# New costs in the scheduler of an attention and two-MLP kernel: loads, small operations, maxima, changes of TensorE's division; the first unit's loads ahead of the third's

## The chip, the cores and the metric

The kernel runs on one core of a Trainium2 chip. A core has five engines that work beside each other, each through its own instructions in order: TensorE (PE, matrix products), VectorE (DVE), ScalarE (ACT), GpSimd (POOL), and SyncE (SP), which here issues loads and stores. The metric is the device time of one execution in microseconds (us). The median is over the runs of a kernel; less is better.

## What is computed

Causal softmax attention is mixed with a linear memory by a gate for each head, and the result goes through two MLPs; all inputs are float32. Here B = 4, H = 8, S = 576, D = 64, and there are B x S = 2304 tokens of 512 numbers.

```python
def _attn_ref(q, k, v, M_prev, z_prev, beta):
    scores = scale * np.matmul(q, k.transpose(0, 1, 3, 2))   # scale = 1 / sqrt(D)
    scores = np.where(causal, -1000000000.0, scores)
    a = np.exp(scores - scores.max(-1, keepdims=True))
    a /= a.sum(-1, keepdims=True) + 1e-09
    local = np.matmul(a, v)
    q_p = phi(q)                                             # phi(x) = (x > 0 ? x : exp(x) - 1) + 1
    mem_ret = np.einsum('bhsd,bhde->bhse', q_p, M_prev)
    mem_norm = np.einsum('bhsd,bhd->bhs', q_p, z_prev)[..., None] + 1e-06
    g = 1.0 / (1.0 + np.exp(-beta))[None, :, None, None]
    return g * (mem_ret / mem_norm) + (1 - g) * local

def _moe_ref(x, w_in, w_out, s, b):         # 512 -> 2048 -> 512
    r = np.maximum(x @ w_in, 0.0)
    return (s * (r * r) + b) @ w_out

def _moe2_ref(x, w_in, w_out, a, b):        # 512 -> 2048 -> 512
    h = x @ w_in
    P = a[0] + a[1] * h + a[2] * h**2 + a[3] * h**3
    Q = 1.0 + np.abs(b[0]) * np.abs(h) + np.abs(b[1]) * h**2
    return (P / (Q + 1e-06)) @ w_out
```

## The kernel before

**The work and its names.** Attention is cut into 32 units: four batches, times two ranges of query rows (rows 0 to 2 and rows 3 to 4, in tiles of 128), times four pairs of heads. A unit with number p loads `q`, `k`, `vm` (v, scaled to `vs` on arrival), `qm` (the queries by rows) and, for two units together, `zb` (z_prev for all partitions). PE forms the scores `s` (line 648), DVE their maxima `st` (655, a custom operation with a second one that reads its accumulator), ACT the exponentials `p` with row sums `rs` (666). PE transposes `p` to `pt` (525), ACT or DVE copies them to `th`, and PE multiplies by `vs` into `av` (857). The memory term goes over `ph` (phi of qm), `tz` = ph x zb (378), the reduction `c` (591), a scaled `ph`, its transpose `pf`, its copy `fs` (for some units also the remainder `fl`), and the last product into `av` (865), which reads `qm` itself as memory. `xp` = av x `cb` (868) ends the unit; `cb` holds reciprocal row sums, for units from 4 on over a round trip through DRAM (store `crow`, load `cb`). Rows of x leave for a DRAM tile `xTd`.

Weights arrive as raw pieces of 128x512 values, two words each (`dAi_0r`, `dAi_1r` of the first MLP's input weights, `dAo0r` to `dAo7r` of its output weights). DVE and ACT decode each: ACT squares (`m`, 418), DVE runs 419, 421, 423 and 425 into `f`; then a high part (`w1ihA`, `w1ohA`, a cast) and a low part (`w1ilA`, `w1olA`, a subtraction at 378) are kept, so that PE multiplies in three passes. `ha` (913) and `acc` (978) are the first MLP's two products for seven blocks of tokens whose x is early; they are mixed into the attention. Activations there are `ra`, `gha` and `gla`. The blocks after them and the whole second MLP follow the attention (`hb`, `ab`, `hc`, `ac`).

**What sets the order.** No order is written by hand. Code adds operations to a plan, each with its due time `at`, the tiles that it reads and writes, and a table `ways` of its cost on each engine that may do it. `Plan.run` then plays the kernel through in its own clock: it takes again and again the operation that can start first (ties go by `at`), on the engine where it would end first, adds its cost to that engine's clock, and frees its consumers after a gap from the table `GAPS`. What comes out is one fixed list of instructions for each engine, which the chip then runs in order; costs never appear in a run, they only decide order and engine. Waits at run time are semaphores on real completions.

Costs come from `ways()` (a base plus columns times a rate), `small()` for operations of a few columns, `pe()` for TensorE, and `load()` for transfers. Most loads go through SP, in order, with a clock step of 0.48 for each; a load of a tile also waits until the buffer's last reader is done, and each of SP's eight queue lanes takes a new load only when the one eight places earlier has landed. The keys of the first units and the gate (`beta`) are loaded by ACT. `gates()` turns beta into `gate`, `omg` and `gate2` by small operations on DVE. PSUM has eight banks: a tile that opens a bank waits until its last reader frees it.

`prepare_qk(p)` loads q and k of a unit, `prepare(p)` its vm, qm and zb. The first three units have their q and k due at TS - AHEAD + 0.001 p, ahead of the rest of their loads; the gate at 0.0005.

Of the kernel before, what the change touches and what calls it, by code (L numbers as in the profile page):

```python
# [20 lines left out]
P = 128  # L21
# [19 lines left out]
PCOPY = False  # L41
RAW = 0
ALONE = 8
R0, R1, RN = 0.0, 0.0, 0
ENDS, LEAD, LEADS = 1, 0.7, 384
WIDTHS = 512, 512, 512, 384, 384
D0, D1, D2, D3 = 10.0, 8.0, 3.0, 0.0
TINYPOOL = 0.12
DIRECT, GATE, MPLAIN = 4, 1.0, 4
# [10 lines left out]
class Op:  # L60


    def __init__(self, ways, fn, at):
        self.ways, self.fn, self.at = ways, fn, at
        self.left, self.next, self.ready, self.end = 0, [], {e: 0.0 for e in ways}, 0.0
        self.touch, self.opens, self.port = [], [], False

# [12 lines left out]
class Plan:  # L80
# [83 lines left out]
    def run(self, engines, nbanks):  # L164
        clock = {e: 0.0 for e in engines}
        wait = {e: [] for e in engines}
        bank_free, bank_of = [0.0] * nbanks, [None] * nbanks
        dma, busy, port = 0.0, [], 0.0
        wait_for = [WAIT_AT]
# [35 lines left out]
        for _ in self.ops:  # L205
            cand = [(c[1], c[2].at, e, c[2], c[3]) for e, c in ((e, choose(e)) for e in engines) if c is not None]
            start, _, e, o, b = min(cand, key=lambda c: c[:2])
            for x in o.ways:
                wait[x].remove(o)
            cost = o.ways[e]  # L210
            if e == "PE":
                busy = [x for x in busy if x[1] > start - 4.0]
                if sum(y - max(x, start - 4.0) for x, y in busy) < 2.6:
                    cost *= 2
                busy.append((start, start + cost))
            elif e != "SP":
                cost *= INFL
            if e == "SP":
                clock[e] = start + 0.48
                dma = max(dma, start + 1.2) + cost  # L220
                o.end = dma + 1.2
            else:
                clock[e] = start + cost
                o.end = clock[e] + o.lag
                if e == "POOL" or e == "DVE" and o.port:
                    port = clock[e]
            for t, i in zip(o.opens, b):
                bank_of[i] = t
                t.obj = self.pools["ps"].tile(t.shape, t.dt, tag=f"bank{i}", name=t.name)
            o.start, o.eng = start, e  # L230
            if o is self.swap:
                wait_for[0] = WAIT
            o.fn(engines[e])
            for t in o.touch:
                t.left -= 1
                t.free = max(t.free, o.end)
                if not t.left and t.place is not None and t.place[0] == "ps":
                    i = bank_of.index(t)
                    bank_of[i], bank_free[i] = None, t.free + BGAP
            for n in o.next:  # L240
# [8 lines left out]
def tile_kernel(ctx, tc, qk, vm, z, beta, w1i, w1o, s1, b1, w2i, w2o, a2, b2, out):  # L249
# [106 lines left out]

    def load(dst, src, size, r=(), w=(), act=False):

        if act:
            op({"ACT": 0.55}, lambda e: e.dma_start(dst(), src()), r, w, lag=1.7 + size / 360e3)  # L360
        else:
            op({"SP": 0.1 + size / 350e3}, lambda e: e.dma_start(dst(), src()), r, w)  # L362
# [17 lines left out]
    def small(fn, r, w, ways_=("DVE", "POOL")):  # L380

        t = {"DVE": 0.07, "POOL": TINYPOOL}
        op({e: t[e] for e in ways_}, fn, r, w, port="POOL" in ways_)

    def pe(cols, fn, r, w, n=0):

        op({"PE": cols * 0.000422 + n * 0.0135}, lambda e: fn(), r, w)

    def gates():

        load(lambda: gate, lambda: beta.rearrange("(o h) -> o h", o=1).to_broadcast([P, H]), 5e3, (), ("gate",), True)
        op(ways(H, 0.0), lambda e: e.activation(gate, gate, AF.Exp, scale=-1.0), ("gate",), ("gate",))
        op(ways(H, None, 1.0), lambda e: e.tensor_scalar(gate, gate, 1.0, None, ALU.add), ("gate",), ("gate",))
        op(ways(H, None, 1.0), lambda e: e.reciprocal(gate, gate), ("gate",), ("gate",))
        op(ways(H, None, 1.0), lambda e: e.tensor_scalar(omg, gate, -1.0, 1.0, ALU.mult, ALU.add), ("gate",), ("omg",))
        op(ways(H, None, 1.0), lambda e: e.tensor_copy(gate2[:, :, 0], gate), ("gate",), (("gate2", 0),))
        for j in range(2):
            m = slice(64 * j, 64 * j + 64)
            op(ways(H, None, 1.0), lambda e, j=j, m=m: e.tensor_copy(gate2[m, j::2, 1], gate[m, j::2]), ("gate",), (("gate2", 1 + j),))


# [136 lines left out]
    def diagonal(p):  # L538

        Q, QD = f"q{p}", f"qd{p % 2}"  # L540
        for j in range(2):
            m = slice(j * D, j * D + D)
            op({"POOL": 0.2}, lambda e, m=m: e.tensor_scalar(g(QD)[m, m], g(Q)[m, P:P + 64], 1.0, 0.0, ALU.mult, ALU.add),
               (Q,), ((QD, j),))

    def prepare(p):
# [6 lines left out]
        if r.ta == 0:  # L553
            load(lambda: g(f"vm{p}")[:, 0:r.kb], lambda: tiles[:, 0:r.kb], P * 512 * r.kb, (), (f"vm{p}",))
            load(lambda: g(f"qm{p}"), lambda: tiles[:, NQ:NQ + 4], P * 512 * 4, (), (f"qm{p}",))
# [66 lines left out]
    def scores(p):  # L622
# [7 lines left out]
        for i, (cols, pieces) in enumerate(r.scores):  # L630
# [6 lines left out]
            for t, x, ka, kb, o in pieces:  # L637
# [11 lines left out]

                pe(4.9 * (kb - ka), mm, (Q, K), [(b, t) for b in banks], 7)  # L650
                for n, b in zip(ns, banks):
# [7 lines left out]
                    ST = (f"st{n}", t)  # L659
                    op(ways(kb - ka, None, 1.0), top, ((b, t), ST) if x else ((b, t),), ((b, t), ST))  # L660
                todo.append((t, x, ka, kb, o, banks, o2))
# [9 lines left out]
    def scores_last(p):  # L671
# [4 lines left out]
        for x in range(2):  # L676
# [4 lines left out]
            def mm(SB=SB, ks=ks):  # L681
                nc.tensor.matmul(g(SB)[:, 0:QB], g(Q), g(K)[:, ks], start=True, stop=True)  # L682

            pe(4.5 * QB, mm, (Q, K), (SB,))
            op(ways(QB, None, 1.0), lambda e, SB=SB, x=x: e.tensor_tensor_reduce(
                g(SB)[:, 0:QB], g(SB)[:, 0:QB], mask2 if x else mask[:, 0:QB], -scale,
# [154 lines left out]
    def values(p, runs):  # L841
# [17 lines left out]

        pe(2 * sum(x[6] - x[5] for x in part) + 50 * len(part), mm, sorted({x[3] for x in part}) + [VS], (AV,))  # L860

# [310 lines left out]
    for j in range(n_early):  # L1172
# [176 lines left out]
```

## Time and profile before

| what | us |
|---|---|
| median of 3 runs (lowest, highest) | 1061.24 (1059.4, 1061.42) |
| the profiled execution, whole time | 1060.15 |
| its span, first to last instruction | 1058.4 |
| busy: PE, DVE, ACT, POOL | 1016.3, 849.0, 687.5, 414.9 |

The span is the part of an execution in which instructions run; 1.75 us of the profiled one lie outside it. A busy time is the sum in which an engine has at least one instruction running. The mean granted clock of TensorE was 0.985 of full speed. The attention with the weight decodes and the first token blocks takes about the first 400 us; the rest is the two MLPs.

### The profile page before, as it was taken

To read this page: it belongs to the slowest core of one execution; us is meant where nothing else is said; L and a number is where in the kernel's file an instruction comes from. 1 tells how busy PE (TensorE), PEld (TensorE's weight loads), DVE (VectorE), ACT (ScalarE), POOL (GpSimd) and SP (SyncE) were. 2 spreads that over 40 slices of the span, in tenths; PEclk is the share of its full clock that TensorE was granted. 3 is DMA by queue.
4 is the path that set the end of the run, shared out by engine and by line. 5 is a ranking of instruction groups with operands and counts; after the bars stand their busy time and mean duration, and the time that the engine had idled before them with its cause. 6 is when DMAs were issued, how large, how long until landed. Compare 5 with 4: busy or idle time off the path is not lost.

```text
span 1058.4 us, 17508 instructions
## 1 busy us (share of the span) xinstructions
PE 1016.3 (96%) x5980; PEld 868.7 (82%) x5980; DVE 849.0 (80%) x1511; ACT 687.5 (65%) x1449; POOL 414.9 (39%) x470
## 2 busy tenths in 40 slices
PE   5886999999999999999999999999999999999998
PEld 3565888878888789987778999888888888898997
DVE  5999987888779885479999543888888888887896
ACT  5866666676557653355554443877866877777895
POOL 2423221032002211012021002877777876876785
PEclk8998999999999999999999999999999999999999
DMA  6666566666656655986765332900200200010000
GB/s 196 203 191 189 150 194 207 170 201 192 192 158 187 181 176 174 365 254 206 254 204 194 102 99 65 325 1 1 78 1 0 70 1 1 23 41 1 30 1 31
DMA packets 88633, 140.42 MB, mean 133 GB/s; under 512 B 12408, under 2 KB 50400, under 8 KB 88544
## 3 DMA queue, kind: packets, MB, share of 16 engines
q1 hardware_dynamic: 83856, 130.52, 39.0%
q0 software_dynamic: 4224, 8.39, 2.5%
q8 instruction: 47, 0.77, 0.3%
q10 hardware_dynamic: 464, 0.40, 0.1%
q14 instruction: 42, 0.34, 0.1%
HBM read 103.56 MB, written 35.71 MB: 132 GB/s over the span
## 4 chain that ended last, share of the span: by engine, by line
PE 71%; DVE 13%; DMA 8%; ACT 3%; issue 2%; SPq 2%; POOL 0%; ACTq 0%; DVEq 0%; POOLq 0%
PE hc L913 19%; PE ac L1104 19%; PE ab L1017 7%; PE hb L913 7%; PE ha L913 6%; PE acc L978 6%; SPq L362 2%; PE av L857 2%; PE pt L525 2%; PE s L648 1%; DVE s L655 1%; DMA cb<-crow 1%; PE av L865 1%; DMA dAi_0r<-in_w1i 1%; PE su L682 1%
## 5 line engine op out<-in xcount | busy, mean ns | idle before, releaser
L1083 DVE RECIPROCAL qe<-qe 128x512 f32<-128x512 f32 (+2 forms) x82 | 242.6, 2959 | 49.4 <-POOL qe L378 49.4
L913 PE MATMUL hc<-xc_h,w2ih 128*128 128x512 f32 (+1 forms) x320 | 117.8, 368 | 0.0
L913 PE MATMUL hc<-xc_h,w2il 128*128 128x512 f32 (+1 forms) x320 | 117.8, 368 | 0.0
L913 PE MATMUL hc<-xc_l,w2ih 128*128 128x512 f32 (+1 forms) x320 | 117.7, 368 | 0.0
L378 POOL TENSOR_TENSOR qe<-qe,qb 128x512 f32<-128x512 f32 (+2 forms) x82 | 94.9, 1158 | 55.1 <-ACT qb L1068 54.2
L1104 PE MATMUL ac<-w2oh,ghc 128*128 128x512 f32 x288 | 112.6, 391 | 0.0
L1104 PE MATMUL ac<-w2ol,ghc 128*128 128x512 f32 x288 | 112.5, 391 | 0.0
L1104 PE MATMUL ac<-w2oh,glc 128*128 128x512 f32 x288 | 112.3, 390 | 0.0
L378 POOL TENSOR_TENSOR glc<-po,ghc 128x512 fp32r<-128x512 f32 (+2 forms) x82 | 95.0, 1158 | 23.2 <-ACT ghc L368 23.1
L378 POOL TENSOR_TENSOR pm<-pm,s 128x512 f32<-128x512 f32 (+2 forms) x82 | 95.3, 1162 | 17.1 <-ACT pm L1068 16.2
L525 PE MATMUL pt<-ident,p 128*128 128x128 f32 x320 | 62.0, 291 | 24.0 <-DVE xp L868 6.8
L1074 ACT ACTIVATE s<-hc 128x512 f32<-128x512 f32 (+2 forms) x82 | 44.6, 544 | 61.2 <-PE hc L913 58.3
L978 PE MATMUL acc<-gha,w1olA 128*128 128x256 f32 x288 | 83.7, 291 | 0.0
L978 PE MATMUL acc<-gla,w1ohA 128*128 128x256 f32 x288 | 81.5, 283 | 0.1
L978 PE MATMUL acc<-gha,w1ohA 128*128 128x256 f32 x288 | 81.3, 282 | 0.0
L666 ACT ACTIVATE p<-s,st 128x128 f32<-128x128 f32 (+3 forms) x128 | 66.5, 526 | 21.7 <-DVE st L655 20.4
L1068 ACT ACTIVATE pm<-hc,prm 128x512 f32<-128x512 f32 (+2 forms) x82 | 59.6, 726 | 22.4 <-DVE hc L1085 21.9
L525 PEld LDWEIGHTS pt<-ident,p 128*128 128x128 f32 x320 | 40.8, 147 | 38.9 <-ACT th L368 8.6
L913 PEld LDWEIGHTS hc<-xc_h,w2il 128*128 128x128 f32 x320 | 60.1, 188 | 9.1 <-DVE po L1087 0.4
L913 PEld LDWEIGHTS hc<-xc_l,w2ih 128*128 128x128 f32 x320 | 60.1, 188 | 8.6
L913 PEld LDWEIGHTS hc<-xc_h,w2ih 128*128 128x128 f32 x320 | 60.0, 188 | 7.4
L1068 ACT ACTIVATE qb<-s,cq,b1abs 128x512 f32<-128x512 f32 (+2 forms) x82 | 62.7, 764 | 2.1 <-POOL qe L378 2.1
(493 smaller groups left out, 2979.8 us busy)
## 6 DMA issues: line engine op xcount, KB each, us to landing
vm<-in_vm SPq DMA_DIRECT2D x16, 384.0 KB
k<-in_qk SPq DMA_DIRECT2D x32, 144.0 KB
x2p<-ev SPq DMA_DIRECT2D x18, 256.0 KB
out_y<-ob SPq DMA_DIRECT2D x18, 256.0 KB
qm<-in_vm SPq DMA_DIRECT2D x16, 256.0 KB
w1d<-sh SPq DMA_DIRECT2D x16, 256.0 KB
w1d<-sl SPq DMA_DIRECT2D x16, 256.0 KB
w2d<-sh SPq DMA_DIRECT2D x16, 256.0 KB
```

Of the source, the lines that this page charges most:

```text
L362: op({"SP": 0.1 + size / 350e3}, lambda e: e.dma_start(dst(), src()), r, w)
L378: op(ways(c, None, dve, pool), lambda e: e.tensor_tensor(dst(), x(), y(), alu), r, w, port=True)
L525: nc.tensor.transpose(dst[:, o:o + P], src, ident)
L666: e.activation(g(f"p{n}_{i}")[:, o:o + kb - ka], g(b)[:, o2:o2 + kb - ka], AF.Exp, scale=-1.0, bias=g(f"st{n}")[:, z_:z_ + 1], accum_out=g ...
L857: nc.tensor.matmul(g(AV)[64 * j:64 * j + 64, ra:rb], g(VS)[:, kb, j], g(TH)[:, o:o + rb - ra], start=x in firsts, stop=False, skip_group_c ...
L913: nc.tensor.matmul(hs(), m, y, start=c == 0 and k == 0, stop=c == KC - 1 and k == 2)
L978: nc.tensor.matmul(a, outp(y, f)[:, cs], g(z_)[:, us], start=f == 0 and k == 0 and c % 2 == 0, stop=f == HF - 1 and k == 2, skip_group_che ...
L1017: nc.tensor.matmul(g(ACC)[:, 0:w], outp(y, f)[:, cs], g(z_), start=f == 0 and k == 0, stop=f == HF - 1 and k == 2)
L1068: return lambda e: e.activation(g(dst)[:, ks], g(src)[:, ks], AF.Identity, scale=m, bias=b)
L1074: op(ways(c, -0.04), lambda e, ks=ks: e.activation(g(S2)[:, ks], g(HS)[:, ks], AF.Square), (HS,), part(S2))
L1083: op({"DVE": 0.07 + c * 0.00625}, lambda e, ks=ks: e.reciprocal(g(QE)[:, ks], g(QE)[:, ks]), part(QE), part(QE))
L1104: nc.tensor.matmul(g(ACC), g(x_)[:, ks], g(f"w2o{y}{i}")[:, o], start=f == 0 and q == 0, stop=f == NF - 1 and q == 2)
```

## The change

The diff changes numbers with which the plan reckons, and the code order of a few loads. No operation is added, taken away or made different.

- Engines' clocks no longer all start at 0 in the plan, but at FIRST (DVE at 2.0, POOL at 3.7). A load costs SP 0.64 instead of 0.48 as long as the plan is before 12 us.
- Small operations cost 0.12 on DVE (0.07 before) and 0.22 on POOL (0.12); maxima cost 0.03 more, those of the last scores 0.06 more; a block of qd costs POOL 0.25 (0.2); a load on ACT costs 0.62 (0.55), the gate's load lands 1.0 later and its exponential costs 1.3 more. The rest of the gate's operations isn't planned before 8.6.
- TensorE operations have a mark `split`: scores "rows", the products with vs "columns", others none. Where the mark changes, unless there was none before, the plan adds 0.2.
- The third unit's q and k are due at 0.02 instead of 0.002, so behind the first unit's `prepare` (0.01). In `prepare`, units with query rows 0 to 2 load vm behind qm and zb instead of ahead of them.

```diff
+FIRST = {"PE": 0.0, "ACT": 0.72, "DVE": 2.0, "POOL": 3.7, "SP": 0.73}
+ISSUE, SLOWLY, UNTIL, TABLE, BEYOND, GATES = 0.48, 0.64, 12.0, 1.3, 1.0, 8.6
...
-TINYPOOL = 0.12
+TINYPOOL, TINYDVE, TOPS, LEAVE = 0.22, 0.12, 0.03, 0.2
...
-        clock = {e: 0.0 for e in engines}
+        clock = dict(FIRST)
...
+                if split is not None and o.split != split:
+                    cost += LEAVE
+                split = o.split
...
-                clock[e] = start + 0.48
+                clock[e] = start + (SLOWLY if start < UNTIL else ISSUE)
...
-            op({"ACT": 0.55}, lambda e: e.dma_start(dst(), src()), r, w, lag=1.7 + size / 360e3)
+            op({"ACT": 0.62}, lambda e: e.dma_start(dst(), src()), r, w, lag=1.7 + late + size / 360e3)
...
-        t = {"DVE": 0.07, "POOL": TINYPOOL}
+        t = {"DVE": TINYDVE, "POOL": TINYPOOL}
...
+        plan.since = GATES
...
-                    op(ways(kb - ka, None, 1.0), top, ((b, t), ST) if x else ((b, t),), ((b, t), ST))
+                    op({"DVE": ways(kb - ka, None, 1.0)["DVE"] + TOPS}, top, ((b, t), ST) if x else ((b, t),), ((b, t), ST))
...
         if r.ta == 0:
-            load(lambda: g(f"vm{p}")[:, 0:r.kb], lambda: tiles[:, 0:r.kb], P * 512 * r.kb, (), (f"vm{p}",))
             load(lambda: g(f"qm{p}"), lambda: tiles[:, NQ:NQ + 4], P * 512 * 4, (), (f"qm{p}",))
...
+        if r.ta == 0:
+            load(lambda: g(f"vm{p}")[:, 0:r.kb], lambda: tiles[:, 0:r.kb], P * 512 * r.kb, (), (f"vm{p}",))
...
-        events.append((t - AHEAD if p >= RQ else TS - AHEAD + 0.001 * p, lambda p=p: prepare_qk(p)))
+        events.append((t - AHEAD if p >= RQ else TS - AHEAD + (0.001, 0.002, 0.02)[p], lambda p=p: prepare_qk(p)))
...
-    plan.at = TS - AHEAD + 0.0005
+    plan.at = TS - AHEAD + 0.0015
```

Three places show how the lists of instructions move; lines of the changed kernel are 5 to 8 higher. TensorE has 5,355 rows of instructions before and after, and the last 3,260 of them are the same in kind.

SP, the program's first loads. Before (a digit in a name is the unit, here 0 to 2, and the number behind it counts tiles):

```order
L362 DMA q0_155<-in_qk 64x384 x2
L362 DMA q1_161<-in_qk 64x384 x2
L362 DMA q2_167<-in_qk 64x384
L362 DMA k2_170<-in_qk 64x384
L362 DMA q2_167<-in_qk 64x384
L362 DMA k2_170<-in_qk 64x384
L362 DMA vm0_176<-in_vm 128x384
L362 DMA qm0_181<-in_vm 128x512
L362 DMA zb0_189<-in_z 128x256
L362 DMA dAi0_0r_195<-in_w1i 128x1024
L362 DMA qm1_202<-in_vm 128x512
```

After:

```order
L367 DMA q0_157<-in_qk 64x384 x2
L367 DMA q1_162<-in_qk 64x384 x2
L367 DMA qm0_168<-in_vm 128x512
L367 DMA zb0_170<-in_z 128x256
L367 DMA vm0_172<-in_vm 128x384
L367 DMA q2_178<-in_qk 64x384
L367 DMA k2_181<-in_qk 64x384
L367 DMA q2_178<-in_qk 64x384
L367 DMA k2_181<-in_qk 64x384
L367 DMA dAi0_0r_205<-in_w1i 128x1024
L367 DMA qm1_210<-in_vm 128x512
```

qm, zb and vm of unit 0 stand ahead of q and k of unit 2, and vm behind zb; the first weight piece stays in its place.

DVE, around the first instruction of the first piece's decode (`dAi0_0f`). The rows ISA on line 655 are the maxima, of unit 0 (`s0`, `s1`) and unit 1 (`s2`, `s3`). Before, from unit 0's last maximum on:

```order
L655 ISA s1_1_0_209,st1_197<-s1_1_0_209,mask_78 128x384
L655 ISA st1_197 128x1
L589 SCALAR_TENSOR_TENSOR ph0_223<-qm0_181,ph0_223 128x384
L655 ISA s2_0_0_225,st2_248<-s2_0_0_225,mask_78 128x128
L655 ISA st2_248 128x1
L378 TENSOR_TENSOR tz0_251<-ph0_223,zb0_189 128x384
L702 TENSOR_SCALAR rs0_200<-rs0_200 128x2x3
L419 TENSOR_SCALAR dAi0_0f_264<-dAi0_0r_195 128x512
L705 RECIPROCAL rec0_95<-rs0_200 128x6
L591 TENSOR_REDUCE c2_0_272<-tz0_251 128x3x2
L421 SCALAR_TENSOR_TENSOR dAi0_0f_264<-dAi0_0r_195,dAi0_0f_264 128x512
```

After, the eleven rows that end with the decode's first instruction:

```order
L663 ISA st1_187 128x1
L599 TENSOR_REDUCE c2_0_243<-tz0_213 128x3x2
L663 ISA s2_0_0_215,st2_253<-s2_0_0_215,mask_78 128x128
L663 ISA st2_253 128x1
L663 ISA s3_0_0_216,st3_256<-s3_0_0_216,mask_78 128x128
L663 ISA st3_256 128x1
L602 RECIPROCAL c2_0_243<-c2_0_243 128x6
L663 ISA s2_0_0_215,st2_253<-s2_0_0_215,mask_78 128x256
L663 ISA st2_253 128x1
L713 RECIPROCAL rec0_95<-rs0_193 128x6
L426 TENSOR_SCALAR dAi0_0f_276<-dAi0_0r_205 128x512
```

tz, the reduction c2_0 and two more maxima of unit 1 (`s3` of 128, `s2` of 256) stand ahead of the first decode instruction; before, the reduction and those maxima stood behind it.

SP, unit 4's round trip of c through DRAM. Before:

```order
L362 DMA crow4_127<-c1_4_914 2x128
L362 DMA crow4_127<-c1_4_914 2x1x64
L362 DMA qm7_934<-in_vm 128x128
L362 DMA qm7_934<-in_vm 64x128 x2
L362 DMA zb4_957<-in_z 128x256
L362 DMA k10_966<-in_qk 64x384
L362 DMA q10_912<-in_qk 64x384
L362 DMA k10_966<-in_qk 64x384
L362 DMA cb4_990<-crow4_127 64x192 x2
```

After:

```order
L367 DMA crow4_127<-c1_4_950 2x128
L367 DMA crow4_127<-c1_4_950 2x1x64
L367 DMA dAi0_1r_972<-in_w1i 128x1024
L367 DMA qm7_940<-in_vm 64x128
L367 DMA zb4_992<-in_z 128x256
L367 DMA cb4_1010<-crow4_127 64x192 x2
```

Between the store crow4 and the load cb4 stood seven loads, and now three.

## Rows read from the trace of the kernel before

**Rows 1.** The page's head: the span and PE's busy time.

```profile
span 1058.4 us, 17508 instructions
...
PE 1016.3 (96%) x5980; PEld 868.7 (82%) x5980; DVE 849.0 (80%) x1511; ACT 687.5 (65%) x1449; POOL 414.9 (39%) x470
```

**Rows 2.** Windows by stage: from:to us, length; busy us (x instructions); PEclk, DMA share, GB/s.

```profile
0.00:16.00 16.00, 7.67 (x38) 5.65 (x38) 6.11 (x30) 5.21 (x16) 3.10 (x15) 0.98 0.68 208
16.00:116.00 100.00, 82.49 (x540) 61.74 (x540) 92.62 (x250) 73.30 (x196) 30.40 (x59) 0.87 0.61 184
116.00:400.00 284.00, 273.78 (x2132) 232.77 (x2132) 230.33 (x690) 184.17 (x503) 53.47 (x109) 0.99 0.60 183
400.00:1050.00 650.00, 647.93 (x3256) 565.27 (x3255) 518.48 (x539) 422.38 (x730) 326.75 (x285) 1.00 0.31 101
```

**Rows 3.** Waits of DVE, 0 to 116 us: total us, times, longest.

```profile
DVE ph L587 <- DMA qm<-in_vm: 3.2, 2, 1.8
DVE tz L378 <- DMA zb<-in_z: 2.7, 1, 2.7
DVE xp L868 <- DMA cb<-crow: 2.0, 1, 2.0
```

**Rows 4.** Waits of PE, 0 to 120 us.

```profile
PE pt L525 <- DVE xp L868: 6.8, 1, 6.8
PE pt L525 <- ACT th L368: 6.4, 2, 5.2
```

**Rows 5.** Timeline of DVE: start, length in us; [idle before it <- its releaser].

```profile
14.70 0.56 DVE L378 TENSOR_TENSOR tz<-ph,zb 128x384 f32<-128x384 f32 x1 [2.73 <-DMA zb<-in_z]
...
16.00 0.43 DVE L419 TENSOR_SCALAR dAi_0f<-dAi_0r 128x512 int32<-128x512 int32 x1 [0.66 <-DMA dAi_0r<-in_w1i]
...
16.44 0.51 DVE L591 TENSOR_REDUCE c<-tz 128x6 f32<-128x384 f32 x1
...
17.54 0.29 DVE L655 CUSTOM_DVE_ANT_0 s<-s,mask 128x128 f32<-128x128 f32 x1
...
18.50 0.43 DVE L655 CUSTOM_DVE_ANT_0 s<-s,mask 128x256 f32<-128x256 f32 x1
...
33.88 0.36 DVE L587 TENSOR_SCALAR ph<-qm 128x384 f32<-128x384 f32 x1 [1.46 <-DMA qm<-in_vm]
...
73.43 0.36 DVE L868 TENSOR_TENSOR xp<-av,cb 128x192 f32<-128x192 f32 x1 [2.05 <-DMA cb<-crow]
...
115.43 0.68 DVE L378 TENSOR_TENSOR w1olA<-dAo7f,w1ohA 128x512 fp32r<-128x512 f32 x1
```

**Rows 6.** Timeline of SP: the issue of three loads.

```profile
7.56 0.44 SPq L362 DMA_DIRECT2D zb<-in_z  x1
...
27.97 0.33 SPq L362 DMA_DIRECT2D qm<-in_vm  x1
...
69.95 1.24 SPq L362 DMA_DIRECT2D cb<-crow  x2
```

**Rows 7.** Timeline of ACT around the first square of a weight piece.

```profile
16.00 0.68 ACT L418 ACTIVATE dAi_0m<-dAi_0r 128x512 f32<-128x512 f32 x1 [3.96 <-DMA dAi_0r<-in_w1i]
16.58 0.36 ACT L666 ACTIVATE p<-s,st 128x128 f32<-128x128 f32 x1
```

**Rows 8.** Timeline of PE: unit 0's last product.

```profile
27.13 0.81 PE L865 MATMUL av<-fs,qm 128*128 128x384 f32 x2
```

**Rows 9.** Timeline of PE: two products of the first MLP.

```profile
90.76 0.28 PE L913 MATMUL ha<-xa0l,w1ihA 128*128 128x256 f32 x1
90.88 0.28 PE L913 MATMUL ha<-xa0h,w1ihA 128*128 128x256 f32 x1
```

**Rows 10.** Waits of PE, 116 to 410 us.

```profile
PE pt L525 <- DVE fl L766: 4.5, 6, 1.4
PE pt L525 <- DVE gla L931: 2.1, 4, 1.4
```

**Rows 11.** Window after PE's longest wait, as rows 2.

```profile
96.00:106.00 10.00, 7.22 (x46) 6.46 (x47) 9.63 (x24) 5.19 (x14) 4.09 (x8) 0.60 0.45 156
```

More of the change, by code (lines that the diff above doesn't have):

```diff
@@ L65, in __init__ @@
         self.left, self.next, self.ready, self.end = 0, [], {e: 0.0 for e in ways}, 0.0
-        self.touch, self.opens, self.port = [], [], False
+        self.touch, self.opens, self.port, self.split = [], [], False, None
 class Buf:
@@ L164, in run @@
     def run(self, engines, nbanks):
-        clock = {e: 0.0 for e in engines}
+        clock = dict(FIRST)
         wait = {e: [] for e in engines}
         bank_free, bank_of = [0.0] * nbanks, [None] * nbanks
-        dma, busy, port = 0.0, [], 0.0
+        dma, busy, port, split = 0.0, [], 0.0, None
         wait_for = [WAIT_AT]
@@ L355, in ways, with load @@
         return t
-    def load(dst, src, size, r=(), w=(), act=False):
+    def load(dst, src, size, r=(), w=(), act=False, late=0.0):
         if act:
-            op({"ACT": 0.55}, lambda e: e.dma_start(dst(), src()), r, w, lag=1.7 + size / 360e3)
+            op({"ACT": 0.62}, lambda e: e.dma_start(dst(), src()), r, w, lag=1.7 + late + size / 360e3)
         else:
@@ L380, in small, with pe @@
     def small(fn, r, w, ways_=("DVE", "POOL")):
-        t = {"DVE": 0.07, "POOL": TINYPOOL}
+        t = {"DVE": TINYDVE, "POOL": TINYPOOL}
         op({e: t[e] for e in ways_}, fn, r, w, port="POOL" in ways_)
-    def pe(cols, fn, r, w, n=0):
-        op({"PE": cols * 0.000422 + n * 0.0135}, lambda e: fn(), r, w)
+    def pe(cols, fn, r, w, n=0, split=None):
+        op({"PE": cols * 0.000422 + n * 0.0135}, lambda e: fn(), r, w).split = split
     def gates():
-        load(lambda: gate, lambda: beta.rearrange("(o h) -> o h", o=1).to_broadcast([P, H]), 5e3, (), ("gate",), True)
-        op(ways(H, 0.0), lambda e: e.activation(gate, gate, AF.Exp, scale=-1.0), ("gate",), ("gate",))
+        load(lambda: gate, lambda: beta.rearrange("(o h) -> o h", o=1).to_broadcast([P, H]), 5e3, (), ("gate",), True, BEYOND)
+        op(ways(H, TABLE), lambda e: e.activation(gate, gate, AF.Exp, scale=-1.0), ("gate",), ("gate",))
+        plan.since = GATES
         op(ways(H, None, 1.0), lambda e: e.tensor_scalar(gate, gate, 1.0, None, ALU.add), ("gate",), ("gate",))
@@ L399, in gates @@
             op(ways(H, None, 1.0), lambda e, j=j, m=m: e.tensor_copy(gate2[m, j::2, 1], gate[m, j::2]), ("gate",), (("gate2", 1 + j),))
+        plan.since = 0.0
     roles = {}
@@ L542, in diagonal @@
             m = slice(j * D, j * D + D)
-            op({"POOL": 0.2}, lambda e, m=m: e.tensor_scalar(g(QD)[m, m], g(Q)[m, P:P + 64], 1.0, 0.0, ALU.mult, ALU.add),
+            op({"POOL": 0.25}, lambda e, m=m: e.tensor_scalar(g(QD)[m, m], g(Q)[m, P:P + 64], 1.0, 0.0, ALU.mult, ALU.add),
                (Q,), ((QD, j),))
@@ L648, in mm @@
                         nc.tensor.matmul(g(b)[:, o2:o2 + kb - ka], g(Q)[m, q], g(K)[m, ka:kb], start=True, stop=True)
-                pe(4.9 * (kb - ka), mm, (Q, K), [(b, t) for b in banks], 7)
+                pe(4.9 * (kb - ka), mm, (Q, K), [(b, t) for b in banks], 7, split="rows")
                 for n, b in zip(ns, banks):
@@ L684, in scores_last @@
             pe(4.5 * QB, mm, (Q, K), (SB,))
-            op(ways(QB, None, 1.0), lambda e, SB=SB, x=x: e.tensor_tensor_reduce(
+            op({"DVE": ways(QB, None, 1.0)["DVE"] + 2 * TOPS}, lambda e, SB=SB, x=x: e.tensor_tensor_reduce(
                 g(SB)[:, 0:QB], g(SB)[:, 0:QB], mask2 if x else mask[:, 0:QB], -scale,
@@ L858, in mm @@
                                  start=x in firsts, stop=False, skip_group_check=True)
-        pe(2 * sum(x[6] - x[5] for x in part) + 50 * len(part), mm, sorted({x[3] for x in part}) + [VS], (AV,))
+        pe(2 * sum(x[6] - x[5] for x in part) + 50 * len(part), mm, sorted({x[3] for x in part}) + [VS], (AV,), split="columns")
         def mem():
```

## Prediction

> **What bounds the kernel now.** I read the busy times first, then the same by stage, then the waits of the two busiest engines in the early stages, and last the order in time around each wait. PE is busy for 1016.3 of 1058.4 us [rows 1]. The stages [rows 2] tell where the other 42 us lie: 8.3 in the first 16 us, 17.5 between 16 and 116 us, 10.2 between 116 and 400, 2 between 400 and 1050, the rest in the tail. So from 400 us on nothing can be gained but by PE doing less, and the change gives PE the same 5,355 rows of instructions. Between 16 and 116 us DVE is busy for 92.6 of 100 us: there VectorE, which decodes the weights beside the attention, sets the end, and PE's gaps are mostly DVE's lateness seen from PE. From 116 us on PE is the bound again, with small gaps. A gain must therefore be (a) time in which DVE waits before 116 us, (b) work that leaves DVE there, or (c) work that PE has already done when that zone ends.
>
> DVE's waits before 116 us that the change touches [rows 3] are 3.2 us for qm, 2.7 for zb, 2.0 for cb. PE's two longest [rows 4] are 6.8 us (a transpose that needs the PSUM bank that xp frees) and 6.4 (transposes that wait for ACT's copies).
>
> **The start.** The profile of before shows DVE idle until 14.70 us for tz, whose zb was asked for at 7.56 us [rows 5, 6]; then, at 16.00, the first weight piece dAi_0r lands, and ACT's copy of unit 0's transposes is queued behind ACT's square of that piece (row dAi_0m: 3.96 us waited) [rows 7]. After the change zb and qm stand third and fourth in SP's queue, so tz, its reduction and three maxima of unit 1 come ahead of the decode's first instruction. dAi_0r stays in place 10, behind the same bytes, and the square still stands ahead of the copies, so I leave the 16.00 where it is. What DVE had to do behind 16.00 and now does before it is the reduction (0.51), a maximum of 128 (0.29) and one of 256 (0.43) [rows 5]: 1.2 us of lead. PE gets less at once: on ACT the exponential that stood between the square and the copies (16.58, 0.36 us) [rows 7] is now ahead of both, so the copies come 0.3 us earlier; but unit 0's last product is then reached without the later waits, and I let it end about 1 us earlier than its 27.13 + 0.81 = 27.94 us [rows 8]. Bounds of the term: 0.3 (the ACT step alone) to 1.2. I take 1.2 for DVE, since DVE sets this zone.
>
> **Unit 2's qm.** Its load is issued at 27.97 us, the moment unit 0's last product (which reads the same buffer) ends at 27.94, and lands at 33.88, where DVE had waited 1.46 us [rows 5, 6, 8]: 5.9 us for 256 KB, with a 512 KB weight piece ahead of it. After, it stands one place later in SP's queue, behind a vm load, but the product ends 1 us earlier and the piece ahead is asked for earlier too. If it still takes 5.9 us from some 26.9 us, it lands at 32.8, and DVE, 1.2 us ahead of 33.88 - 1.46 = 32.4, is there at 31.2: the wait stays at 1.5, and DVE keeps only 1.1 of lead. If it comes much sooner, the 1.46 us go as well. I take 1.0 us of it, because most of those 5.9 us went to the bytes ahead, and keep 0 and 1.46.
>
> A rule bears on this term. The Trainium skill (DMA: Bandwidth & Descriptors, Anatomy of one DMA) gives about 2.0 us plus the bytes over 436 KB per us for one transfer by GpSimd's software queue, an estimate of 2.6 us here. The row shows more than twice that, in a loaded queue; by the page the wait would vanish and the sum be 0.5 us lower, by the row it would stay and the sum be 1.0 higher.
>
> **cb of unit 4.** DVE waits 2.05 us for it at 73.43, and its load was issued at 69.95 [rows 5, 6]. Between the store that it reads and cb itself stood seven loads on SP; now three. A load takes SP 0.4 to 0.6 us (zb 0.44, cb 1.24 for two) [rows 6], so cb is asked for about 2 us earlier relative to its store. I take 1.5, between 0 (a queue lane that must first land an older load holds SP) and 2.05.
>
> **DVE's share of the work.** The planner also hands out movable operations anew, because small ones and maxima now cost DVE more in its tables. Counted up to the last first-layer decode (115.43 us before), DVE has one 512-wide two-input operation less (0.68 us, as w1olA) and two 384-wide products ph less (0.56 each, as tz) [rows 5]; against that stand two 256-wide products, a reduction, two scalings and an ml more, and a copy th, a copy rb and a cast less, together about 0.9 us more. Net 0.9 us less. Bounds: 0 to 1.8. Zero is real: what leaves DVE goes to POOL, which is slower at it and may run beside DVE's own two-input operations.
>
> **PE's place at the end of that zone.** When PE comes to unit 9's first scores, it has by the order done 12 ha products more and 6 transposes more, and one 256-wide and one 384-wide score product less. A ha product takes 0.12 us from start to start [rows 9]; a transpose I put at the same, the two scores at 0.35 together (estimates from that row, by columns). 18 x 0.12 - 0.35 = 1.8 us of PE's work are moved into gaps that DVE had left. This counts in full only if PE is never held afterwards; I take half, 0.9, with 0 and 1.8 as bounds.
>
> **The 6.8 us stall.** Before, PE had six ha products between unit 6's last product and the transpose that needs the bank; after, it has two score products, twelve ha and ten products of the next unit's av, some 4 us by my estimate. xp, however, stands behind much the same decodes on DVE. The gap shrinks as seen from PE, but what PE does there it lacks later in the same DVE-bound zone; it is the previous term seen from another side, and I count it once.
>
> **New waits.** Each term takes slack out of somewhere, and landings that the plan misjudged before it can misjudge at other places. DVE's three waits named above made 7.9 us; I charge a quarter of that, 2.0 us, for waits that I can't name, between 0 and 5.5 (all the gains named, which new waits would then eat).
>
> **The sum.** 1.2 + 1.0 + 1.5 + 0.9 + 0.9 - 2.0 = 3.5 us. Against the profiled execution, 1060.15 us (a span of 1058.4 and 1.75 around it), that is 1056.7. The median shown is 1061.24, 1.1 us above the profiled one; halfway between the two references gives 1057.2 us. From no change a measurement of this kernel can tell about 0.2%, 2.1 us.
>
> **Rivals.**
>
> *The gain is swallowed.* The zone is bound by DVE, dAi_0r still lands at 16.00, and the leads are only earlier arrivals at loads that come when they come: qm takes its 5.9 us, the lanes hold cb, and only content and half a microsecond of start are left. 0.3 + 0 + 0 + 0.9 + 0.9 - 1.0 = 1.1 less: 1059.6 from the same starting point (1060.7). For it: all three of DVE's named waits are for transfers, whose landing no order sets; against it: they are asked for earlier in the new order. Chance 0.22.
>
> *Slower.* PE's order from 116 to 400 us is dealt anew, too, and PE is in order: a transpose that waits for fl or gla from DVE holds all that stands behind it. Before, six waits for fl and four for gla cost 4.5 and 2.1 us [rows 10], 0.66 each; DVE is at 81% there [rows 2], so a new order can put PE closer to DVE. If that order has twelve more of them, 8 us, the 5.5 us of named gains are lost and 2.5 more, 1063.2. It decides from nine more on (5.9 us): then it is slower than before. For it: the order there is chosen by a table whose small DVE operations now cost more, which makes the plan's DVE later and its PE no faster; against it: the same table should then leave PE more room. Chance 0.18.
>
> *Larger gain.* PE runs at a granted clock of 0.60 between 96 and 106 us, 7.2 us of busy time [rows 11], right after the 6.8 us without work; of the two levels, 1.2 and 2.4 GHz, this is mostly the lower. If the 4 us of work that now stand in the gap keep the clock up, about 3 us of these 7.2 (what lies above 0.60 x 7.2 = 4.3) come back, provided that DVE has left the zone by then. 3.5 + 3 = 6.5 less: 1054.2, and with all terms at their upper bounds and no new waits, 1.2 + 1.5 + 2.05 + 1.8 + 1.8 = 8.4, 1052.3. Against it: DVE is busy for nearly all of this stretch. Chance 0.12. The Trainium skill (TensorE: Matmul & The Clock Gate, Terms) puts such a penalty at the throttled time times one minus the ratio of the clocks, an estimate of 4 to 5 us for 10 us, more than the 3 us that I read from the row; by it this case would end near 1052.5.
>
> **Chances and range.** The forecast 0.48, larger gain 0.12, swallowed 0.22, slower 0.18. Faster than 1059.1: 0.60; within 2.1 us of 1061.24: 0.22; slower: 0.18. The likeliest case alone spans 1054 to 1059. The range that leaves out no more than 2 in 10 reaches from 1052 (upper bounds) to 1063 (half of the slower case).
>
> **What would show it.** tz right behind qm's product well before 14 us and DVE without the 2.7 us wait; dAi_0f still at about 16.0; unit 2's qm landing no later than 32.8; DVE's wait for cb under 0.6 us; the last first-layer decode (w1olA from dAo7f) at 111 to 114 us rather than 115.43; PE's busy share between 116 and 400 us no lower than now. I am wrong if dAi_0r lands at another time than 16.0 (the whole start follows it), if a new wait of 3 us or more stands on DVE before 116 us, or if PE's idle time from 116 to 400 us grows beyond 15 us.

## The result, and the profile after

The changed kernel takes 1066.50 us (median of 6 runs, 1064.77 to 1069.70) where the kernel before takes 1059.69 (6 runs, 1057.11 to 1061.42): a ratio of 1.0070, with an interval of 1.0047 to 1.0092. It is 6.8 us slower; I had forecast 1057.2 and a gain. The profiled execution took 1066.82 us. Lines of the changed kernel are 5 to 8 higher than before.

The page's head, which answers to [rows 1]:

```profile
span 1065.0 us, 17532 instructions
...
PE 1019.6 (96%) x5980; PEld 868.4 (82%) x5980; DVE 840.6 (79%) x1501; ACT 690.8 (65%) x1462; POOL 414.8 (39%) x467
```

The windows by stage, with the columns of [rows 2]:

```profile
0.00:16.00 16.00, 10.26 (x44) 6.90 (x44) 9.86 (x47) 8.29 (x26) 5.02 (x20) 0.89 0.75 227
16.00:116.00 100.00, 83.54 (x592) 62.97 (x592) 93.67 (x266) 76.90 (x212) 30.05 (x57) 0.98 0.64 190
116.00:400.00 284.00, 267.20 (x2014) 224.07 (x2015) 216.05 (x647) 179.94 (x494) 52.17 (x103) 0.98 0.60 180
400.00:1050.00 650.00, 647.57 (x3284) 565.62 (x3283) 515.80 (x535) 418.83 (x717) 322.56 (x278) 1.00 0.31 101
```

By 116 us the changed kernel has done 636 of PE's matmuls, 58 more than before (578). Between 116 and 400 us it does 118 fewer (2014 for 2132), and PE is idle for 284.0 - 267.2 = 16.8 us there instead of 10.2. So there was a gain, larger than I forecast, and it was lost behind the decodes. Cut at the moments at which units 7, 15 and 31 end (the start of their xp on DVE), the same view shows where; first the changed kernel:

```profile
0.00:108.15 108.15, 86.09 (x580) 63.77 (x580) 96.58 (x284) 79.23 (x215) 32.52 (x72) 0.97 0.67 200
108.15:204.35 96.20, 91.60 (x697) 76.31 (x698) 76.64 (x240) 62.80 (x173) 21.82 (x39) 1.00 0.61 181
204.35:415.99 211.64, 199.30 (x1522) 169.15 (x1522) 150.51 (x445) 128.02 (x348) 32.90 (x69) 0.98 0.56 167
415.99:1065.00 649.01, 642.64 (x3185) 559.16 (x3184) 516.86 (x536) 420.74 (x726) 327.59 (x287) 1.00 0.31 102
```

and the kernel before, cut at the same four units:

```profile
0.00:116.50 116.50, 90.24 (x578) 67.39 (x578) 99.23 (x282) 78.90 (x213) 33.51 (x74) 0.88 0.62 187
116.50:208.07 91.57, 89.62 (x708) 76.58 (x709) 75.22 (x236) 61.42 (x173) 17.59 (x39) 1.00 0.62 189
208.07:409.69 201.62, 193.77 (x1514) 165.52 (x1513) 157.31 (x459) 126.40 (x338) 35.88 (x70) 0.99 0.58 176
409.69:1058.40 648.71, 642.63 (x3185) 559.23 (x3184) 517.22 (x536) 420.80 (x726) 327.90 (x287) 1.00 0.31 102
```

The lengths differ by -8.35, +4.63, +10.02 and +0.30 us, together the 6.6 by which the spans differ. Units 16 to 31 carry nearly the same number of matmuls (1522 for 1514) and take 10 us longer: 4.5 more idle time (12.34 for 7.85) and 5.5 more busy time.

**The early part.** The timeline of DVE, at the places of [rows 5]:

```profile
9.10 0.56 DVE L383 TENSOR_TENSOR tz<-ph,zb 128x384 f32<-128x384 f32 x1
...
13.04 0.39 DVE L426 TENSOR_SCALAR dAi_0f<-dAi_0r 128x512 int32<-128x512 int32 x1
...
29.50 0.36 DVE L595 TENSOR_SCALAR ph<-qm 128x384 f32<-128x384 f32 x1 [1.28 <-DMA qm<-in_vm]
...
67.30 0.35 DVE L876 TENSOR_TENSOR xp<-av,cb 128x192 f32<-128x192 f32 x1
...
106.78 0.68 DVE L383 TENSOR_TENSOR w1olA<-dAo7f,w1ohA 128x512 fp32r<-128x512 f32 x1
```

tz no longer waits and comes 5.6 us earlier. The last decode is 8.65 us earlier. ACT's first square shows when the first piece landed, against 16.00 in [rows 7]:

```profile
12.88 0.68 ACT L425 ACTIVATE dAi_0m<-dAi_0r 128x512 f32<-128x512 f32 x1 [0.33 <-DMA dAi_0r<-in_w1i]
```

**Behind the decodes.** PE's waits from 116 to 410 us, which answer to [rows 10]:

```profile
PE pt L532 <- DVE fl L774: 6.6, 7, 1.9
PE pt L532 <- DVE gla L939: 2.4, 2, 2.0
PE su L690 <- DVE th L375: 1.5, 1, 1.5
PE su L690 <- ACT th L373: 1.3, 2, 1.0
PE s L656 <- DVE xp L876: 1.3, 1, 1.3
```

The transposes wait for fl and gla 9 times (before 10), 1.0 us each on average instead of 0.66, and the waits for th in this stretch sum to 4.0 us, where they were 0.8. One of these stalls, in the order of time. SP asks for a piece of the second MLP's weights (timeline of SP):

```profile
202.78 0.42 SPq L367 DMA_DIRECT2D dB_1r<-in_w1o  x1
```

DVE stands 2.89 us for it, decodes it, and comes to fl behind the decode (timeline of DVE):

```profile
207.90 0.43 DVE L426 TENSOR_SCALAR dB_1f<-dB_1r 128x512 int32<-128x512 int32 x1 [2.89 <-DMA dB_1r<-in_w1o]
...
211.31 0.68 DVE L383 TENSOR_TENSOR sl<-dB_1f,sh 128x512 fp32r<-128x512 f32 x1
211.91 0.55 DVE L774 TENSOR_TENSOR fl<-pf,fs 128x384 fp32r<-128x384 f32 x1
```

and PE, in the timeline of PE, stands for fl, and behind it runs products at half speed:

```profile
212.61 0.52 PE L532 MATMUL pt<-ident,p 128*128 128x128 f32 x3 [1.86 <-DVE fl L774]
...
213.39 0.42 PE L986 MATMUL acc<-gha,w1olA 128*128 128x256 f32 x1
213.60 0.41 PE L986 MATMUL acc<-gla,w1ohA 128*128 128x256 f32 x1
```

A product acc starts 0.21 us after the one ahead of it, where ahead of the stall it was 0.12 (from 210.35 to 210.47 us). Such stretches, the lower of the two levels (1.2 GHz), are three in units 16 to 31; windows of the changed kernel:

```profile
213.20:216.60 3.40, 3.40 (x19) 3.40 (x18) 2.40 (x9) 3.03 (x11) 0.00 (x0) 0.50 0.71 191
267.80:271.20 3.40, 3.40 (x19) 3.40 (x18) 3.33 (x12) 2.23 (x6) 1.27 (x3) 0.51 0.81 268
383.90:387.30 3.40, 3.40 (x21) 2.68 (x21) 3.29 (x10) 2.06 (x5) 1.60 (x2) 0.50 0.61 177
```

10.2 us at a granted clock of 0.50 are 5.1 us of PE's work not done. The Trainium skill (TensorE: Matmul & The Clock Gate, Terms) reckons such a penalty in the same way. The trace agrees as far as the spacing of the products, 0.21 for 0.12 us, tells. Before there was one such stretch in these units:

```profile
377.00:380.40 3.40, 3.40 (x18) 3.40 (x18) 3.33 (x11) 3.35 (x11) 0.00 (x0) 0.50 0.18 33
```

So of the 5.5 us by which PE is busy longer in units 16 to 31, the clock accounts for some 3.4 (5.1 less 1.7). Where the other 2 come from, no run shows.

### The profile page after: what moved, and what is told of

The parts are those of the page before. It is cut to its first block, busy times and chain, and to the rows that moved or that the text cites. A ratio compares the mean times of both kernels' runs of the same rounds, so it can differ in the third digit from the quotient of the medians.

```text
span 1065.0 us, 17532 instructions
## 1 busy us (share of the span) xinstructions
PE 1019.6 (96%) x5980; PEld 868.4 (82%) x5980; DVE 840.6 (79%) x1501; ACT 690.8 (65%) x1462; POOL 414.8 (39%) x467
## 4 chain that ended last, share of the span: by engine, by line
PE 67%; DVE 16%; DMA 9%; issue 3%; ACT 2%; SPq 1%; POOL 0%; ACTq 0%; DVEq 0%; POOLq 0%
PE hc L921 19%; PE ac L1112 19%; PE ha L921 6%; PE acc L986 6%; PE ab L1025 5%; PE hb L921 4%; PE av L865 2%; PE s L656 2%; SPq L367 1%; PE pt L532 1%; DMA dB_0r<-in_w1i 1%; DMA qm<-in_vm 1%; DMA dB_2r<-in_w1o 1%; DVE s L663 1%; DVE hb L938 1%
## 5 line engine op out<-in xcount | busy, mean ns | idle before, releaser
L663 DVE CUSTOM_DVE_ANT_0 s<-s,mask 128x128 f32<-128x128 f32 (+3 forms) x128 | 60.5, 507 | 7.0 <-PE s L656 6.2
```

The lines of the kernel that those rows point to most:

```text
L663: e.tensor_tensor_reduce(sp, sp, mask[:, m0:m0 + kb - ka], -scale, 3.0e38 if x == 0 else st[:, t:t + 1], ALU.add, ALU.min, st[:, t + x:t + ...
```

## The experiments

**The theories.** A: the order that the new table deals behind the first layer's decodes costs what the start gains, and more. B: the lead is given back whatever stands behind it, because loads come when they come. C: within A, the loads of the second MLP's weights stand too late in SP's new list; DVE's waits for them sum to 9.2 us before and 17.5 after (116 to 420 us). D: one of the table's numbers is to blame.

**Half of each order.** The scheduler takes its own choice up to a step CUT, and from there the recorded list of the other kernel, with its engines:

```diff
-            start, _, e, o, b = min(cand, key=lambda c: c[:2])
+            start, _, e, o, b = min(cand, key=lambda c: c[:2]) if step < CUT else follow()
```

`follow()` returns the first operation of that list that is not done, has its inputs, and finds its banks free. The cut is the decode w1olA of dAo7. e1_new_start_old_rest has the changed kernel's order up to there and the order of before behind it (CUT = 736):

> Changed kernel up to the last first-layer decode (there it was 8.65 us ahead), and from there every remaining operation in the order and on the engine that the kernel before gave it. If the new order behind that point is what costs (theory), the lead of 8 to 9 us stays: about 1051 us against 1059.7. If an early lead cannot be kept, whatever the order behind it (rival: the attention stage gives it back), it ends at 1059 to 1062.

1053.76 us, a ratio to before of 0.9932 (0.9904 to 0.9960). e2_old_start_new_rest is the reverse (CUT = 734):

> The other way round: the kernel before up to its last first-layer decode, then the order of the changed kernel. Theory: the rest costs about 14 to 15 us wherever it starts, so about 1073 us. Rival (lead given back): without a lead nothing is given back, 1060 to 1062.

1077.56 us, 1.0176 (1.0136 to 1.0217). The new order ahead of the cut gains, and the new order behind it costs 13 us (the change against e1) to 18 us (e2 against before): A stands, and B, that the whole lead goes whatever stands behind it, falls. Windows of e1, cut at the same units:

```profile
0.00:112.26 112.26, 89.76 (x581) 65.32 (x581) 96.94 (x282) 78.51 (x215) 32.99 (x73) 0.92 0.64 193
112.26:206.44 94.18, 90.59 (x706) 76.22 (x707) 75.56 (x236) 61.44 (x173) 17.39 (x38) 1.00 0.61 185
206.44:403.93 197.49, 190.72 (x1512) 163.26 (x1512) 156.91 (x459) 126.52 (x338) 35.16 (x70) 1.00 0.59 179
```

Units 16 to 31 take 197.49 us, 14 less than in the changed kernel, at a clock of 1.00. In units 8 to 15 B holds in part: e1 has the order of before there and takes 94.18 us for 91.57, so 2.6 of the 4.2 us by which it was ahead at the end of unit 7 are given back. That e1 ends 5.8 us ahead is also due to units 16 to 31, which run 4 us faster than before in the same order. PE's waits for fl in e1, 116 to 410 us:

```profile
PE pt L559 <- DVE fl L801: 6.0, 6, 1.5
```

They are hardly less than the changed kernel's 6.6, so the sum of this wait doesn't tell the two apart. The longest of them is 1.5 us here and 1.9 there, and none is followed by a stretch at the lower clock here; that this is what makes the difference is not shown.

**Parts of the diff.** In the kernels of this part the numbers of the table that are left out stand as before. e3_start_and_loads_only keeps FIRST, SLOWLY, GATES, the gate's numbers and the order of the loads:

```diff
-TINYPOOL, TINYDVE, TOPS, LEAVE = 0.22, 0.12, 0.03, 0.2
+TINYPOOL, TINYDVE, TOPS, LEAVE = 0.12, 0.07, 0.0, 0.0
```

> The kernel before with only the start's part of the change: engines' first times, SP's slower issue, the gate's lateness, ACT's load cost, and the order of the loads. If the worse rest comes from the numbers for small operations, maxima and divisions, this keeps the gain: 1050 to 1054. If any touch of the table deals the rest anew and the outcome is a matter of chance (rival), it lies anywhere between 1050 and 1070, and not at 1059.7 minus what the other part costs.

1057.89 us, 0.9987 (0.9970 to 1.0004). e4_small_tops_leave_only is its complement, with the clocks, SP's costs and the loads of before:

```diff
-FIRST = {"PE": 0.0, "ACT": 0.72, "DVE": 2.0, "POOL": 3.7, "SP": 0.73}
+FIRST = {"PE": 0.0, "ACT": 0.0, "DVE": 0.0, "POOL": 0.0, "SP": 0.0}
```

> The kernel before with only the costs of small operations, maxima, qd and changes of division. If those numbers make the rest worse, this loses 12 to 15 us without the early gain: about 1072 to 1075. If it is chance, anywhere between 1050 and 1070.

1078.66 us, 1.0180 (1.0151 to 1.0208). So the loss comes with small operations, maxima and LEAVE. Single ones, or pairs, beside e3's part (the last row is the changed kernel itself; the fourth to sixth columns tell which of the numbers are the new ones):

| kernel | us | ratio (interval) | small | maxima | LEAVE |
|---|---|---|---|---|---|
| e10_start_and_small | 1057.80 | 1.0004 (0.9984 to 1.0023) | new | | |
| e9_start_and_maxima | 1055.18 | 0.9971 (0.9953 to 0.9990) | | new | |
| e11_start_and_leave | 1054.11 | 0.9958 (0.9946 to 0.9971) | | | new |
| e5_without_leave | 1064.65 | 1.0055 (1.0032 to 1.0077) | new | new | |
| e12_without_small | 1067.53 | 1.0095 (1.0067 to 1.0123) | | new | new |
| the change | 1066.50 | 1.0070 (1.0047 to 1.0092) | new | new | new |

Their edits are the same line with other numbers; e11's, for one:

```diff
-TINYPOOL, TINYDVE, TOPS, LEAVE = 0.22, 0.12, 0.03, 0.2
+TINYPOOL, TINYDVE, TOPS, LEAVE = 0.12, 0.07, 0.0, 0.2
```

> Start and loads, and of the numbers only those of small operations (DVE 0.12, POOL 0.22, qd 0.25). If the small operations make the rest worse: 1063 to 1070. If the maxima do: 1055 to 1060.

> Start and loads, and of the numbers only TOPS (a maximum 0.03 dearer). Start and loads alone took 1057.9 us, with small operations and maxima 1064.65. If the dearer maxima make the rest worse: 1063 to 1067. If the small operations do: 1055 to 1060. A deal anew by an immaterial number has so far moved times by 2 to 3.6 us, so under 4 us is no verdict.

> Start and loads, and of the numbers only LEAVE. It took 1.85 us off when it was left out of the whole change, within the scatter of a new deal: so 1055 to 1061 here, near the 1057.9 of start and loads alone. Over 1063 would mean that LEAVE does cost, and that the test without it was masked by the others.

> The change without the 0.2 for a changed division (LEAVE = 0). Theory that LEAVE is what makes the rest worse: the early gain stays and the loss goes, 1052 to 1057 us. Rival (small operations and maxima do it): 1064 to 1070, as the whole change. Rival (chance): anywhere from 1052 to 1075.

> The whole change without the numbers for small operations. If those numbers make the rest worse: 1055 to 1061. If maxima or LEAVE do: 1063 to 1070.

No single number costs anything; maxima with either of the others do (small operations with LEAVE alone were not tried). The dearer maxima are in every slow kernel of this part, and by themselves, in e9, they are harmless. D falls: the numbers act only through the order that they deal together.

**A number that says nothing.** To see what a new dealing is worth by itself, TOPS is moved by 0.001 us: e6_after_tops_0_031 in the changed kernel, e7_start_only_tops_0_001 in e3, e8_before_tops_0_001 in the kernel before.

```diff
-TINYPOOL, TINYDVE, TOPS, LEAVE = 0.22, 0.12, 0.03, 0.2
+TINYPOOL, TINYDVE, TOPS, LEAVE = 0.22, 0.12, 0.031, 0.2
```

> The changed kernel with the cost of a maximum raised by one more thousandth (TOPS 0.031 for 0.03), which no engine can notice, but which deals the order anew from DVE's row 123 on. If the numbers themselves cause the loss, it stays at 1064 to 1069. If the order that comes out is a matter of chance, it differs from 1066.5 by more than 3 us, either way.

> Start and loads only, with 0.001 added to each maximum, an immaterial number that deals the order anew from DVE's row 122 on. If numbers cause times: 1056 to 1060, as with start and loads only (1057.9). If chance: differs by more than 3 us.

> The kernel before with 0.001 added to each maximum, which deals its order anew from DVE's row 116 on. If numbers cause times: 1058 to 1061.5. If the order before was one draw among many and a good one: slower by 3 us or more.

1068.53 us, 1.0088 (1.0057 to 1.0119); 1055.90, 0.9970 (0.9948 to 0.9991); 1062.64, 1.0026 (1.0004 to 1.0047). Against the kernels that they vary these are +2.0, -2.0 and +3.6 us; the first two lie within the intervals, the third doesn't. A thousandth of a microsecond in a table was worth 3.6 us on the chip in one of three cases (0.4 to 5.0 by the interval). Effects of 2 us among the rows of the table above therefore say nothing about the numbers as such; the 6 to 19 us by which the bad ones are slower than before are more than these three edits moved.

**The weights' loads (C).** Every list of instructions is word for word that of the kernel named, but for the 16 loads of `dB` pieces, which stand 3 to 10 places earlier in SP's list, or, in e15, up to 6 places later. One of them, in e13_after_weights_earlier, in SP's list:

```diff
 DMA xTd<-xp 128x384
+DMA dB_0_1r<-in_w1i 128x1024
 DMA q<-in_qk 64x192
 DMA k<-in_qk 64x576
 DMA q<-in_qk 64x192
 DMA k<-in_qk 64x576
 DMA xa2r<-xTd 128x2x192
 DMA q<-in_qk 64x192
 DMA k<-in_qk 64x576
-DMA dB_0_1r<-in_w1i 128x1024
```

> The changed kernel, with each of the 16 loads of the second half's weight pieces 3 to 10 places earlier in SP's list, and nothing else moved. If DVE and ACT held by these pieces are what costs: DVE's waits for dB (17.6 us in the trace) fall under 4, and the time falls to 1054 to 1060. If the loss lies in the order of PE, DVE and ACT itself: 1064 to 1068.

> The same move in the kernel before, whose DVE waits 9.4 us for these pieces. If the wait costs about as much for each us: 1053 to 1057. If its waits there are hidden: 1058 to 1061.

> The kernel before with these loads up to 6 places later in SP's list (at most 4 us in the plan). If the late pieces cause the loss: DVE's waits for them double or more, and the time rises to 1066 to 1080. If they don't: 1058 to 1063.

> New start and old rest (1053.8 us), with the loads earlier. If the wait costs: 1047 to 1051. If not: 1052 to 1055.

| kernel | lists of | loads | us | ratio (interval) |
|---|---|---|---|---|
| e13_after_weights_earlier | the change | earlier | 1065.17 | 1.0044 (1.0019 to 1.0069) |
| e14_before_weights_earlier | before | earlier | 1056.76 | 0.9969 (0.9944 to 0.9994) |
| e15_before_weights_later | before | later | 1103.35 | 1.0435 (1.0381 to 1.0490) |
| e16_best_weights_earlier | e1 | earlier | 1050.06 | 0.9915 (0.9888 to 0.9942) |

DVE's waits for `dB` pieces are gone from the traces of e13, e14 and e16, and sum to 48.5 us in e15 in the same stretch. Late weights can cost much: e15 loses 43 us. But they are not the change's loss: without any such wait e13 is still 5.2 us slower than before, and the same edit took 3.2 us off the kernel before (e14). Between the two kernels the ratios lie 0.0075 apart with the loads earlier, 0.0070 without. e13's window over units 16 to 31, and its longest waits on PE from 116 to 410 us:

```profile
208.29:415.94 207.65, 195.61 (x1522) 166.86 (x1522) 150.66 (x444) 128.11 (x348) 34.00 (x69) 0.98 0.55 168
```

```profile
PE pt L559 <- DVE fl L801: 5.0, 5, 3.2
PE s L683 <- issue: 2.4, 1, 2.4
PE pt L559 <- DVE gla L966: 2.1, 2, 1.7
```

207.65 us instead of 211.64, with PE idle for 12.0 as before the edit (12.3). The stall for fl moved and became longer, 3.2 us. C is at most a small part. e17_after_weights_and_x_earlier moves loads of early x (`xa`) ahead as well:

```diff
+DMA xa2r<-xTd 128x2x192
 DMA vm<-in_vm 128x768
 DMA qm<-in_vm 64x128
 DMA zb<-in_z 128x256
-DMA xa2r<-xTd 128x2x192
```

> The changed kernel with the 16 weight loads (as e13) and the 20 loads of x for the token blocks behind 100 us up to 19 places earlier in SP's list, all other lists word for word. If the loads that hold DVE and ACT are most of the loss: 1055 to 1060. If the order of the engines is: 1062 to 1067, near e13's 1065.17. An x load that waits on SP for its store can also hold SP, which would make it slower.

1072.00 us, 1.0136 (1.0094 to 1.0179): slower. Its waits of SP from 116 to 410 us show where it stands, and under them DVE's:

```profile
SPq L394 <- DMA xTd<-xp: 33.5, 11, 5.7
```

```profile
DVE xp L903 <- DMA cb<-crow: 20.6, 11, 4.8
```

A load of x needs the store xTd to have landed; asked for earlier, it holds SP (33.5 us, 15.0 in the changed kernel), and what stands behind it on SP, cb among them, comes later (20.6 us for 5.9).

**Where in the order.** e18_new_until_unit_15 keeps the changed kernel's order up to unit 15's xp and goes on with that of before (the splice of e1 with CUT = 1425):

```diff
-CUT = 736
+CUT = 1425
```

> The changed kernel up to unit 15's xp, then the order of the kernel before. If the loss lies in the new order of units 16 to 31: 1052 to 1056, as new start and old rest (1053.76). If what the new order did before unit 16 makes the later loss: 1060 to 1067.

1059.70 us, 1.0006 (0.9987 to 1.0026). It lies apart from e1 (0.9932) and from the change (1.0070): the new order costs something up to unit 15, and again in units 16 to 31. How the loss divides isn't settled. The medians put about half in each, 0.0074 and 0.0064, or 7.8 and 6.8 us. The traces put most of it in units 16 to 31; windows of e18 over units 8 to 15 and 16 to 31:

```profile
109.31:207.37 98.06, 92.17 (x697) 77.25 (x698) 77.05 (x240) 63.05 (x173) 21.86 (x39) 0.98 0.59 178
207.37:406.92 199.55, 192.58 (x1522) 164.79 (x1522) 154.87 (x453) 125.68 (x337) 36.13 (x71) 1.00 0.58 177
```

With the new start, units 8 to 15 take 96.20 and 98.06 us in the new order (the change, e18) and 94.18 in the old one (e1): 2 to 4 us. Units 16 to 31 take 207.7 to 214.4 us in the four traces with the new order (the change, e2, e13, e17) and 195.6 to 201.6 in the five with the old one (before, e1, e14, e16, e18); the two groups do not overlap. What makes it a bad order, as a rule that one could read off a list, the runs did not settle.

## Why the prediction was wrong

**The direction.** The step that failed is the one called new waits: "I charge a quarter of that, 2.0 us, for waits that I can't name, between 0 and 5.5." Behind unit 7 the changed kernel loses 4.6 + 10.0 = 14.6 us. I had sized the charge by the three waits of DVE that the change removes, which has nothing to do with what a new order may cost, and the bound of 5.5 was the sum of the gains, no bound at all. The range ended at 1063 for the same reason. In its place the runs show two things: a new order of units 16 to 31 that is slower in all four traces (10.0 us in the change), and in units 8 to 15 a loss of 4.6 us, of which e1 has 2.6 with the order of before.

**The swallowed-gain rival** fits a part of that last loss. Where the order of before stands in units 8 to 15, the kernel that comes there earlier takes longer for them: e1 94.18 us for before's 91.57, e16 97.00 for e14's 92.54. But it had nearly the whole lead lost in that way, and e1 ends 5.8 us below before.

**The slower rival** had the place right (116 to 400 us, PE in order behind DVE), and the condition that I named, idle time beyond 15 us, held: 16.8. Its price was wrong in kind. It counted twelve more waits for fl and gla; there is one fewer. The waits are longer, others (of su, for th) stand beside them, and some are followed by stretches at half the clock, which I had priced only as a gain.

**The start** was too small. I left the first piece at 16.0 us, since it stands in the same place of SP's list; it landed by 12.9. In all the kernels here with the new order of the first loads ACT reads it at 12.5 to 14.2, in those with the old order at 14.7 to 16.0, so it is the order of the loads ahead of it that counts. Why they delay the piece less in the new order, no run isolates. Unit 0's last product starts at 22.46 instead of 27.13 [rows 8], where I had let it gain 1 us.

**qm of unit 2** came as the row said: it was issued at 23.54 and DVE went on at 29.50, 6.0 us, and the wait stayed at 1.28 (forecast 1.5). An estimate by the Trainium skill (DMA: Bandwidth & Descriptors, Anatomy of one DMA), 2.6 us for these bytes by a fit for GpSimd's queue, would have removed it; this load goes through SP, and the measurement decides for the row. **cb of unit 4** is not waited for any more (67.30), as forecast.

**The lead** at the last decode is 8.65 us in the traces shown; I had said 1.4 to 4.4. It is not all the order's, and part of its size is luck: with the same order up to there e1 has this decode at 111.05, e13 at 110.11 and e18 at 107.94 us, and with the order of before e15 has it at 112.52 and e14 at 116.95. One execution differs from another by some 4 us in this part. The six traces with the new order (the change, e1, e13, e16, e17, e18) average 108.7 us, the four with the old one (before, e2, e14, e15) 114.8: a lead of about 6. The larger-gain rival's mechanism is in it: the granted clock from 16 to 116 us is 0.98, where it was 0.87 [rows 2]. PE's 6.8 us stall [rows 4] became 3.7.

**DVE's content** was sized too small. Until unit 7 ends DVE is busy for 96.58 us instead of 99.23, 2.65 less, where I had 0.9 and at most 1.8; the other 5.7 of the 8.35 us are idle time (11.57 for 17.27), where the start, qm and cb were to give 3.7.

**PE's place** can't be read from the 58 matmuls more by 116 us, since these are the lead itself: when unit 7 ends PE has done 580 for 578. What the 18 products that I counted were worth, no run isolates.

**The signs of being wrong** all came. The first piece landed at another time, PE's idle time passed 15 us, and DVE has a wait of over 3 us before 116 us that it did not have: 4.19 us for the first scores, at 6.14 us. This one cost nothing, since before DVE stood 3.41 us there for the gate and reached its first maximum at 6.33.

## What to carry to other kernels

A list scheduler's table is not a set of independent knobs: each edit deals the whole order anew, and on the chip that is worth several us in either direction, whatever the number's truth. So price a change of such a table in two parts, the places that it is meant for and a spread for all the rest, and take the spread from runs of like edits, not from the waits that the change removes. Edits of a thousandth are not enough for that: here they moved the time by 2 to 3.6 us, and edits of the size of the change's numbers by -5 to +19. Where the parts can be spliced, keep the part of the order that measured better: e1 and e16, at 1053.76 and 1050.06 us, beat both kernels.

## What I had not expected of the hardware

- A stall of about 2 us on PE cost nearly as much again behind it: after 1.86 us for fl the granted clock was 0.50 for 3.4 us, and products started every 0.21 us instead of every 0.12. The stretch from 267.8 us followed two shorter waits, 1.03 us (su, at 265.12) and 0.97 us (for fl, at 267.53). It isn't always so: in e14 PE stood 2.13 us for gla until 351.64, and the granted clock was 1.00 from 351 to 356 us.
- A piece of 512 KB asked for at 202.78 us was there at 207.90, and 256 KB asked for at 23.54 at 29.50: among other transfers the smaller one took longer.
- The same instructions, in the same order, reach the last decode between 106.78 us (the change) and 111.05 us (e1).
